# Attention and routed expert layers in one kernel: the attention stage reordered, its evictions widened to two banks, and some transposes moved from TensorE to the DMA queues

## The chip, the cores and the metric

The kernel runs on one core of one Trainium2 chip. The metric is the device time of one execution in microseconds (us). Five runs of the kernel before gave a median of 749.58 us (748.85 to 750.01). The profiled executions that are quoted have a span, first to last instruction, of about 2 us less than the time.

## The reference, cut to what matters

Two parts follow each other. Block attention with a learned mixing of the blocks of keys and values comes first:

```python
B, H, S, D = 4, 8, 768, 64          # 32 heads, handled as 16 pairs; 8 blocks of 96 rows
P = sort_net                         # 8x8 per head
for _ in range(5):                   # five times: max, exp, normalise rows, normalise columns
    P = np.exp(P - P.max(-1, keepdims=True))
    P = P / (P.sum(-1, keepdims=True) + 1e-09)
    P = P / (P.sum(-2, keepdims=True) + 1e-09)
k_sorted = einsum('bhij,bhjcd->bhicd', P, k_blocks)     # and v_sorted likewise
attn = softmax(q_blocks @ k_sorted.T / sqrt(D))
attn_out = attn @ v_sorted
```

Its output, transposed to 3072 rows of 512, feeds eight experts of which every row uses all, weighted by a matrix that is normalised eight times:

```python
P = exp(x @ w_gate - max);  8 x: rows to 1, columns to 1, times N / E
out = sum over e of P[:, e] * (relu(x @ w1[e]) @ w2[e])     # N 3072, D 512, F 1024, E 8
```

The expert layers are 3072 matmuls of 128x128 weights on 512 columns. They dominate.

## The kernel before: the parts that matter

A step `m` of the attention stage works on four pairs at once, each one stage further: it sorts keys and values of pair m and transposes its queries, takes scores of pair m-1, mixes values for pair m-2, and transposes the result of pair m-3. From step 7 on the first batch is complete and expert blocks (`fill`) stand between the stages. Until then a filler matmul (`spin`) stands there.

```python
    def bank(shape, dt=F32):                     # one PSUM bank, eight in rotation
        return ps.tile(shape, dt, name="bank")

    for it in range(5):                          # prologue, 32x64 each, VectorE and ScalarE in turn
        nc.scalar.activation(out=P, in_=P, func=AF.Exp)
        ...
            nc.vector.tensor_tensor(out=Prep, ...)          # last: 32x1024, every entry 16 times
    # [cut: 8 small matmuls, Pbig, R of pair 0 on VectorE]

    def fill(n, both=True):
        for _ in range(n):
            ...
            if last_batch[c] > state["done"]:
                if state["done"] < 0:
                    spin(1)                      # a matmul whose result nobody reads
                return
            h_block(e, c, fb, both)              # 4 matmuls of 512 columns and a relu
            state["h"] += 1

    for m in range(NPAIR + 4):
        if m < NPAIR:
            stage1(m)          # K: 12 matmuls, V: 12, Q: 12 transposes; each bank evicted by itself
        # [cut: loads of pair m+4, expert weights]
        fill(1)
        if 1 <= m <= NPAIR:
            stage2(m - 1)      # scores: 16 matmuls, 4 exponentials of 96x384; V: 8 transposes
        fill(1)
        if 2 <= m <= NPAIR + 1:
            stage3(m - 2)      # mix: 16 matmuls, 4 x (reciprocal, product) on VectorE
        fill(1)
        # [cut: gate]
        if 3 <= m <= NPAIR + 2:
            stage4(m - 3)      # output: 8 transposes, one copy on ScalarE
        fill(1)
        if m >= 6 and m % 4 == 2:
            state["done"] = m // 4 - 1
```

The softmax here doesn't subtract the row's maximum and nothing guards it: scores larger than these inputs give would overflow.

## Time and profile before

| What | us | Where it is read |
|---|---|---|
| span | 747.3 | head of the page |
| TensorE (PE) busy | 736.2 (99%) | page, part 1 |
| first attention matmul | 14.35 | timeline |
| start of step 7, from where expert work fills every gap | 42.42 | timeline |
| first second-layer matmul, after attention and routing | 145.61 | timeline |
| one second-layer tile, 8 matmuls of 512 columns | 1.727 | distance of VectorE's evictions in the timeline |

From the page of the kernel before: the line of busy times of part 1 and the first line of part 4, the chain that ended last.

```profile
PE 736.2 (99%) x4588; PEld 357.4 (48%) x4588; DVE 252.0 (34%) x497; ACT 274.2 (37%) x497; POOL 48.9 (7%) x71
...
PE 98%; DMA 1%; POOL 1%; DVE 0%; issue 0%; POOLq 0%
```

TensorE is the engine that everything waits for, so what counts is the order of time on TensorE. The next fence is from the windows view of the kernel before (columns: stretch in us, its length, busy time and instructions of PE, PE weight loads, VectorE = DVE, ScalarE = ACT, GpSimd = POOL, then the granted clock, the busy share of the DMA engines and GB/s).

```profile
10.00:15.00 5.00, 1.04 (x22) 1.06 (x24) 3.32 (x11) 0.34 (x2) 3.66 (x6) 0.64 1.30 198
15.00:20.00 5.00, 5.00 (x83) 3.12 (x81) 2.31 (x5) 2.40 (x6) 3.75 (x6) 0.68 1.43 199
30.00:40.00 10.00, 9.98 (x219) 7.86 (x215) 9.38 (x29) 8.49 (x20) 6.68 (x10) 1.00 1.31 203
```

Two things stand out. From 10 to 20 us the granted clock is 0.64 and 0.68, so TensorE ran at half speed for part of it (the first K, at 14.35 us, took 0.59 us to the start of V, the next, at 18.23 us, 0.36). And from 30 to 40 us VectorE is busy for 9.38 of 10 us while TensorE is busy for all of it, but partly with fillers. Here is step 5 of the kernel before (steps count from 0), TensorE's rows of the timeline, two fillers left out (start in us, modelled duration, matmuls merged by line; L171 sorts keys and values, L182 transposes queries, L197 are scores, L204 the V transposes, L216 the mix, L227 the output transposes, L266 fillers):

```profile
33.99 0.53 PE L171 MATMUL bank<-R,kb 128*64 128x128 bf16 x12
34.35 0.50 PE L171 MATMUL bank<-R,vb 128*64 128x128 bf16 x12
34.69 0.50 PE L182 MATMUL bank<-ident,qb 128*64 128x128 bf16 x12
35.12 0.39 PE L266 MATMUL bank<-wide 128*128 128x512 bf16 x1
35.44 0.56 PE L197 MATMUL bank<-QT,KT 64*96 64x96 bf16 x16
35.93 0.65 PE L204 MATMUL bank<-ident,VT 128*96 128x128 bf16 x8
...
36.63 0.87 PE L216 MATMUL bank<-vs,at 96*96 96x65 bf16 x16
37.34 0.38 PE L266 MATMUL bank<-wide 128*128 128x512 bf16 x1
37.56 0.50 PE L227 MATMUL bank<-ident,OG 96*128 96x96 bf16 x8
```

The modelled durations overlap; what a group costs TensorE is the distance from its start to the next start. Here that is 0.36 us for K, 0.34 for V, 0.43 for Q, 0.49 for scores and 0.48 for V transposes, 0.71 for the mix, 0.34 for the output: 3.15 us of 4.22. The rest is fillers and gaps.

### The profile page before, as it was taken

What the parts mean: (1) busy time and instruction counts of PE and PEld (TensorE: products, weight loads), DVE (VectorE), ACT (ScalarE), POOL (GpSimd) and SP (SyncE); (2) the same over time, 40 slices, a digit from 0 to 9 for tenths busy, and PEclk for the clock granted to TensorE, in tenths of its full rate; (3) what the DMA queues carried; (4) which work ended last, traced back from release to release, by engine and by line L of the source; (5) the groups of instructions that cost most, each with busy time, mean ns of one, the idle gap of its engine ahead of it and who ended that gap; (6) DMA issues with size and microseconds to landing.
All of it is one profiled execution on the core that took longest, in us unless ns stands there. A gap on an engine that the chain in (4) does not pass through costs nothing.

```text
span 747.3 us, 10663 instructions
## 1 busy us (share of the span) xinstructions
PE 736.2 (99%) x4588; PEld 357.4 (48%) x4588; DVE 252.0 (34%) x497; ACT 274.2 (37%) x497; POOL 48.9 (7%) x71
## 2 busy tenths in 40 slices
PE   6999999999999999999999999999999999999997
PEld 3776665444444444444444444444444444444443
DVE  5887776632122122221221221221221222212443
ACT  2867665513423324324324334234233233243000
POOL 8542000000000000000000000000000000000000
PEclk8999999999999999999999999999999999999999
DMA  9999000011300061200330033000330003000133
GB/s 148 204 205 173 11 2 0 1 29 29 56 1 1 0 104 28 38 1 1 56 57 1 0 57 45 13 0 1 57 56 1 1 0 57 1 0 1 43 154 141
DMA packets 29679, 33.21 MB, mean 44 GB/s; under 512 B 1984, under 2 KB 22464, under 8 KB 29632
## 3 DMA queue, kind: packets, MB, share of 16 engines
q0 software_dynamic: 26128, 26.23, 22.4%
q1 hardware_dynamic: 3504, 6.30, 2.2%
q8 instruction: 36, 0.59, 0.3%
q14 instruction: 11, 0.09, 0.0%
HBM read 52.45 MB, written 6.29 MB: 79 GB/s over the span
## 4 chain that ended last, share of the span: by engine, by line
PE 98%; DMA 1%; POOL 1%; DVE 0%; issue 0%; POOLq 0%
PE bank L249 45%; PE bank L339 44%; PE bank L171 2%; PE bank L216 2%; PE bank L204 1%; PE bank L197 1%; PE bank L266 1%; DMA qb<-in_q_dram 1%; PE bank L182 1%; PE bank L227 1%; PE bank L236 0%; POOL kb L87 0%; POOL vb L87 0%; PE bank L321 0%; POOL qb L87 0%; DVE osbl L345 0%
## 5 line engine op out<-in xcount | busy, mean ns | idle before, releaser
L255 ACT ACTIVATE hTs<-bank 128x512 bf16<-128x512 f32 x358 | 213.7, 597 | 371.2 <-PE bank L249 370.4
L249 PE MATMUL bank<-xtT,w1e 128*128 128x512 bf16 x1536 | 346.1, 379 | 0.0
L339 PE MATMUL bank<-w2e,hTs 128*128 128x512 bf16 x1536 | 338.0, 379 | 0.0
L345 DVE SCALAR_TENSOR_TENSOR osbl<-bank,glog,osbl 128x512 f32<-128x512 f32 x168 | 126.2, 751 | 398.7 <-PE bank L339 398.7
L339 PEld LDWEIGHTS <-hTs 128*128 128x128 bf16 x1536 | 150.2, 98 | 181.1
L249 PEld LDWEIGHTS <-w1e 128*128 128x128 bf16 x1536 | 147.9, 98 | 170.3
L342 DVE TENSOR_SCALAR osbl<-bank,glog 128x512 f32<-128x512 f32 x24 | 18.0, 751 | 54.7 <-PE bank L339 54.7
L200 ACT ACTIVATE at<-bank 96x384 bf16<-96x384 f32 x64 | 26.0, 487 | 7.9 <-PE bank L197 7.6
L220 DVE TENSOR_TENSOR OG<-bank,rc 96x256 bf16<-96x256 f32 x64 | 26.9, 421 | 2.2
L95 POOL DMA_DIRECT2D w1e<-in_moe_w_dram x8 | 6.0, 752 | 312.6 <-PE bank L249 312.3
L99 POOL DMA_DIRECT2D w2e<-in_moe_w_dram x8 | 7.1, 887 | 237.6 <-PE bank L339 237.1
L253 DVE TENSOR_SCALAR hTs<-bank 128x512 bf16<-128x512 f32 x26 | 17.8, 683 | 6.1 <-PE bank L249 6.1
L229 ACT COPY xtT<-bank 128x768 bf16<-128x768 bf16 x16 | 12.8, 798 | 14.1 <-PE bank L227 13.7
L176 ACT CAST KT<-bank 128x384 bf16<-128x384 f32 x32 | 13.8, 486 | 7.9 <-PE bank L171 7.8
L216 PEld LDWEIGHTS <-at 96*96 96x96 bf16 x256 | 14.1, 125 | 2.8
L216 PE MATMUL bank<-vs,at 96*96 96x65 bf16 x256 | 14.0, 209 | 0.0
L87 POOL DMA_DIRECT2D kb<-in_k_dram x16 | 11.6, 724 | 17.4 <-PE bank L171 16.2
L178 DVE CAST VT<-bank 128x384 bf16<-128x384 f32 x16 | 8.9, 553 | 10.6 <-PE bank L171 8.2
L207 DVE COPY vs<-bank 96x1024 bf16<-96x1024 bf16 x16 | 11.0, 690 | 4.0 <-PE bank L204 3.7
L219 DVE RECIPROCAL rc<-bank 96x4 f32<-96x4 f32 x64 | 10.9, 171 | 3.7 <-PE bank L216 3.7
L87 POOL DMA_DIRECT2D vb<-in_v_dram x16 | 11.6, 725 | 6.9 <-PE bank L171 3.4
L87 POOL DMA_DIRECT2D qb<-in_q_dram x16 | 11.6, 724 | 2.7 <-PE bank L216 1.2
(57 smaller groups left out, 184.4 us busy)
## 6 DMA issues: line engine op xcount, KB each, us to landing
w1e<-in_moe_w_dram POOLq DMA_DIRECT2D x8, 1024.0 KB, 8.0
w2e<-in_moe_w_dram POOLq DMA_DIRECT2D x8, 1024.0 KB, 8.8
out_dram<-osbl SPq DMA_DIRECT2D x24, 256.0 KB, 2.0
kb<-in_k_dram POOLq DMA_DIRECT2D x16, 192.0 KB, 7.4
vb<-in_v_dram POOLq DMA_DIRECT2D x16, 192.0 KB, 7.4
qb<-in_q_dram POOLq DMA_DIRECT2D x16, 192.0 KB, 7.4
P<-in_sort_net_dram SPq DMA_DIRECT2D x1, 8.0 KB, 1.6
wg<-in_moe_w_gate_dram POOLq DMA_DIRECT2D x1, 8.0 KB, 6.7
```

Source lines behind the costliest of these rows:

```text
L87: nc.gpsimd.dma_start(out=t, in_=src[2 * m:2 * m + 2].rearrange("h p kk d -> p h kk d"))
L171: nc.tensor.matmul(b_[64 * h2:64 * h2 + 64, k3, :], src[:, h2, 3 * kh2 + k3, :], R[:, h2].rearrange("p i c -> p (i c)"), start=True, stop= ...
L176: nc.scalar.copy(dst, b_)
L200: nc.scalar.activation(out=ATT[m][h2][:, half, :], in_=bb[h2].rearrange("k i q -> k (i q)"), func=AF.Exp, scale=scale)
L216: nc.tensor.matmul(b_[:, i4, :], ATT[m][h2][:, half, 96 * i4:96 * i4 + 96], VS[m][:, i, h2, :], start=True, stop=True)
L220: nc.vector.tensor_tensor(out=OG[m][:, 4 * half:4 * half + 4, h2, :], in0=b_[:, :, 0:64], in1=mkap(rc, [rc.ap[0], [1, 4], [0, 64]]), op=AL ...
L249: nc.tensor.matmul(b_, w1t[e][:, kk, fb * 128:(fb + 1) * 128], xf[:, kk, c * 512:(c + 1) * 512], start=(kk == 0), stop=(kk == 3))
L253: nc.vector.tensor_scalar_max(hT[e, c][:, fb, :], b_, 0.0)
L255: nc.scalar.activation(out=hT[e, c][:, fb, :], in_=b_, func=AF.Relu)
L339: nc.tensor.matmul(b_, hT[e, c][:, fb, tt * 128:(tt + 1) * 128], w2t[e][:, fb, :], start=(fb == 0), stop=(fb == 7))
L342: nc.vector.tensor_scalar(out=osbl[:, t, :], in0=b_, scalar1=glog[:, t, e:e + 1], scalar2=None, op0=ALU.mult)
L345: nc.vector.scalar_tensor_tensor(out=osbl[:, t, :], in0=b_, scalar=glog[:, t, e:e + 1], in1=osbl[:, t, :], op0=ALU.mult, op1=ALU.add)
```

## The change

Its intent is to shorten all that is not expert work: a shorter prologue with the clock kept up, cheaper evictions in steps 0 to 6 and no fillers after step 1, and for the last six pairs fewer transposes on TensorE. The diff, cut to its core:

```diff
+    QA = 2; MB = 10; XB = 10; VA = 3            # [written on lines of their own]
+    SPIN = [(1, 1, 1, 1)] * 2 + [(0, 0, 0, 0)] * 5
+    PROG = ["KF0VFSvF1XQF"] * 7 + ["KVQFSvF01FXF"] * 3 + ["VKQFSvF01FXF"] * 10
-    ps = ... bufs=8 ...                          # one tile per bank
+    PS = ps.tile([128, 8, 512], F32)             # all of PSUM, bank() and bank2() slice it
+    def bank2():                                 # two neighbouring banks
+        turn[0] += turn[0] % 2
+        b_ = PS[:, turn[0] % 8:turn[0] % 8 + 2, :]
...
-    nc.vector.reduce_max(out=rs, in_=P, axis=AX.X)      # and the subtraction
+        if it == 2:
+            q_turn(0, "act")                     # query transposes of pairs 0 and 1 in the prologue
+            spin(12)
+        if it == 4:
+            q_turn(1, "act")
+            spin(8)
-            nc.vector.tensor_tensor(out=Prep, ...)       # 32x1024
+    nc.tensor.matmul(b_, Pb..., ident[0:32, 0:32], ...)  # transpose, then spread by 8 small matmuls
+    build_r(0, pbp..., nc.vector)                        # R of pairs 0 and 1; from pair 2 on: nc.gpsimd
...
+        b2 = bank2().rearrange("d f x -> d (f x)")       # K and V: one eviction of 768 columns
+            nc.scalar.copy(T[:, 0:VA], b2[:, 0:VA])      # V: half each
+            nc.vector.tensor_copy(T[:, VA:6], b2[:, VA:6])
...
+        else:                                            # m >= MB: V sorted by 2 matmuls of 384 columns,
+            vd[m] = drp.tile([6, 128, 128], BF16, ...)   # written to DRAM and read back turned
+            nc.sync.dma_start(out=vd[m]..., in_=VR...)
...
+            nc.scalar.activation(out=ATT[m][h2], in_=bb[h2], func=AF.Exp, scale=scale)   # 96x768
...
+    def x_back(m):                                       # m >= XB: output to DRAM, back transposed
+            nc.sync.dma_start_transpose(out=xr[m], in_=xd[m])
...
+    early = [..., (0, 1, 0, 256), (1, 1, 0, 256), (0, 1, 256, 512), (1, 1, 256, 512), ...]  # half blocks
...
+            y_tile(e, c, tt, 2 if n == len(seq) - 1 and tt == 3 else 1)    # last tile in halves
```

The letters of `PROG` are the order within a step: K, V, Q sort and turn, S scores, v V transposes, 0 and 1 the mixes of the two heads, X output, F an expert block or a filler.

## The prediction

> **What bounds the kernel now.** TensorE, almost everywhere. Page part 1: PE busy 736.2 of 747.3 us; chain of waits: PE 98%. In the last tiles (timeline) VectorE evictions follow every 1.7268 us, eight 512-column matmuls, so 215.9 ns each. The 3072 expert matmuls are then 663 us of pure streaming, which the change does not shorten. All gains lie in the other 84 us:
> - Prologue: the first attention matmul starts at 14.35 us (timeline), after five normalisations of about 1.81 us, a 1.21 us Prep, Pbig and R. The windows view shows a granted clock of 0.64 and 0.68 from 10 to 20 us, costing some 1.5 us more.
> - Pairs 0 to 6, no expert work yet: step 7 starts at 42.42 us, the first expert matmul at 43.55. Steps take 4.2 to 4.4 us, of which matmuls about 3.15 (K .36, V .33, Q .43, scores .49, V transposes .49, mix .71, output transposes .34). The rest is 28 filler matmuls and gaps. VectorE is 94% busy from 30 to 40 us, ScalarE 85%: VectorE sets this pace.
> - From step 7 on PE is 100% busy; a step is 6.80 us: 16 expert matmuls (3.45), attention 3.14, gaps 0.2.
> - Tail after the last matmul: about 4 us.
>
> **What the change does.**
> 1. Prologue: no maximum and subtraction (0.45 us), no 1.21 us Prep; two small matmul steps instead; R of pair 0 straight from PSUM; queries first, two transposed while the chain runs; fillers keep the clock up. The Trainium skill ("TensorE: Matmul & The Clock Gate", section "What's actually happening") says an idle array drops to half clock; the 0.64 agrees. First attention matmul near 13.0 us, at full clock.
> 2. Steps 0 to 6: two-bank evictions halve the fixed costs (the 96x384 exp took 487 ns, the 128x512 relu 597; I estimate 0.75 us per 768 columns), R moves to GpSimd, the fillers of steps 2 to 6 go. Estimated per step: VectorE 4.4 to 3.45 us, ScalarE 3.65 to 3.35, TensorE 3.15 plus 0.3 to 0.5 of gaps. Pace 3.6 to 3.8. The loads land at about 1 us each, 3 per pair, plus about 5 for a first-layer weight load, so pair 6 lands near 31 us: close, just not binding. Step 7 starts near 35.8: 6.6 us gained, including item 1.
> 3. Pairs 10 to 15: V transposes (0.49) and output transposes (0.34) leave TensorE for the DMA: 6 x 0.83 = 5.0 us, all critical because PE is full there. The round trips have 6 us and more of slack.
> 4. Costs: 96 expert matmuls become 192 of half width (estimated +0.7 us), some new bank waits.
> 5. Tail: last tile in halves, -0.5 us.
>
> Sum: -6.6 -5.0 +0.7 -0.5 = -11.4 us.
>
> **Predicted: 738.2 us, range 735 to 743. Faster by over 2%: 0.09; within 2%: 0.89; slower: 0.02.**
>
> **What would show it.** First attention matmul at 13.0 us, clock near 1 from 10 to 20; step 7 near 36 us; steps 7 to 9 still about 6.8 us, steps 10 to 15 about 6.0; expert matmuls at 216 ns; PE idle still small.
>
> **What would make it wrong.** The DMA transpose being slow, or the SyncE queue blocking, so that VectorE's copy of the result waits and holds PE; GpSimd behind on R because its load issues stall; loads binding at step 6; more gaps from changing matmul tile shapes more often; half-width matmuls costing more than half.

## The result

| | median us | range | runs |
|---|---|---|---|
| before | 749.12 | 748.79 to 750.01 | 13 |
| changed | 740.82 | 739.47 to 741.62 | 7 |

The ratio is 0.9884 (95% interval 0.9874 to 0.9894). It is the mean time of one kernel's fast runs over that of the other's of the same rounds, so not quite the ratio of the medians. The record lists an eighth run of the changed kernel, 743.18 us at a mean clock of 0.995, also called fast, which the median of seven leaves out; the median of all eight would be the same, but this run lies just above the forecast range. The gain is 8.3 us of the medians, clear of noise and within 2%. The time lies within the forecast range of 735 to 743; the forecast gain was 11.4 us.

The same two lines of the changed kernel's page:

```profile
PE 730.8 (99%) x4523; PEld 361.8 (49%) x4523; DVE 239.4 (32%) x425; ACT 271.3 (37%) x460; POOL 62.2 (8%) x96
...
PE 97%; DMA 1%; DVE 1%; issue 0%; POOL 0%; ACT 0%; POOLq 0%; DVEq 0%; ACTq 0%
```

The busy share says nothing: it was 99% and is 99%. Two of the three stretches in the changed kernel:

```profile
10.00:15.00 5.00, 4.08 (x55) 2.44 (x55) 2.37 (x9) 1.48 (x2) 2.37 (x5) 1.00 1.30 197
...
30.00:40.00 10.00, 9.74 (x210) 8.04 (x210) 8.84 (x19) 7.93 (x12) 8.39 (x13) 1.00 1.28 204
```

The clock is now 1.00, and VectorE is busy for 8.84 instead of 9.38 us although steps are shorter. This is step 3 of the changed kernel (L222 sorts keys or values, L284 is the mix of one head, L264 scores, L274 V transposes, L317 output, L147 queries), a step that nothing disturbed:

```profile
22.77 0.53 PE L222 MATMUL PS<-R,kb 128*64 128x128 bf16 x12
23.23 0.55 PE L284 MATMUL PS<-vs,at 96*96 96x65 bf16 x8
23.70 0.53 PE L222 MATMUL PS<-R,vb 128*64 128x128 bf16 x12
24.16 0.60 PE L264 MATMUL PS<-QT,KT 64*96 64x96 bf16 x16
24.81 0.61 PE L274 MATMUL PS<-ident,VT 128*96 128x128 bf16 x8
...
26.11 0.53 PE L147 MATMUL PS<-ident,qb 128*64 128x128 bf16 x12
26.46 0.50 PE L222 MATMUL PS<-R,kb 128*64 128x128 bf16 x12
```

The step takes 3.69 us. K and V now cost 0.46 each: about 0.1 us more, since a group of another tile shape follows each of them. (Not every change of shape costs this: the mix of the second head takes 0.34 us before the output, less than the first takes before V.) Scores cost 0.65 instead of 0.49, though the V transposes follow them in both kernels. That is at least partly a wait: the V transposes start at 24.81 us, just after VectorE's product of the first mix (24.07 to 24.76 us in VectorE's timeline), whose bank they are next to use. But step 4 took 4.35 us, and step 7 started later than expected. Part of the reason is in these rows of the same view, from steps 4 and 6:

```profile
27.83 0.60 PE L264 MATMUL PS<-QT,KT 64*96 64x96 bf16 x15
29.01 0.24 PE L264 MATMUL PS<-QT,KT 64*96 64x96 bf16 x1 [0.59 <-issue]
...
34.47 0.34 PE L222 MATMUL PS<-R,kb 128*64 128x128 bf16 x6
35.02 0.36 PE L222 MATMUL PS<-R,kb 128*64 128x128 bf16 x6 [0.20 <-issue]
```

The sixteenth score matmul and the second half of K came late, and the profile names no engine that they waited for ("issue").

Two points on TensorE, the start of step 7 and the first second-layer matmul (141.29 us in the changed kernel), divide the two traces into three stretches, which account for the whole difference of the spans, 747.3 and 739.0 us. The changed kernel runs one expert block (0.96 us) at the end of step 6; its first stretch is counted to the start of that block. With it, it runs four expert blocks more (16 matmuls at 215.9 ns, 3.45 us) before the second layer; they are taken from the second stretch and added to the third.

| Stretch | before | changed | gain | forecast |
|---|---|---|---|---|
| start to step 7 | 42.42 | 39.60 - 0.96 = 38.64 | 3.8 | 6.6 |
| step 7 to the first second-layer matmul | 103.19 | 102.65 - 3.45 = 99.20 | 4.0 | 5.0 - 0.7 = 4.3 |
| the second layer to the end | 601.7 | 597.7 + 3.45 = 601.2 | 0.5 | 0.5 |

So the forecast missed by 2.8 us in the first stretch, and nearly nowhere else. That the second stretch fits is partly luck: there the DMA route gave about 0.7 us less than forecast and the half-width blocks cost about 0.4 us less (experiment 1), and these two misses nearly cancel.

### The profile page after: what moved, and what is told of

It reads as the page before. It is cut to its first block, busy times and chain, and to the rows that moved or that the text cites. A ratio compares the mean times of both kernels' runs of the same rounds, so it can differ in the third digit from the quotient of the medians.

```text
span 739.0 us, 10546 instructions
## 1 busy us (share of the span) xinstructions
PE 730.8 (99%) x4523; PEld 361.8 (49%) x4523; DVE 239.4 (32%) x425; ACT 271.3 (37%) x460; POOL 62.2 (8%) x96
## 4 chain that ended last, share of the span: by engine, by line
PE 97%; DMA 1%; DVE 1%; issue 0%; POOL 0%; ACT 0%; POOLq 0%; DVEq 0%; ACTq 0%
PE PS L339 45%; PE PS L454 45%; PE PS L284 2%; PE PS L222 1%; PE PS L264 1%; DMA qb<-in_q_dram 1%; PE PS L274 1%; PE PS L147 1%; PE PS L138 0%; PE PS L317 0%; PE PS L326 0%; PE PS L244 0%; DVE OG L288 0%; PE PS L432 0%; DVE VT L230 0%
## 5 line engine op out<-in xcount | busy, mean ns | idle before, releaser
L345 ACT ACTIVATE hTs<-PS 128x512 bf16<-128x512 f32 (+1 forms) x372 | 215.1, 579 | 390.8 <-PE PS L339 389.9
L339 PE MATMUL PS<-xtT,w1e 128*128 128x512 bf16 (+1 forms) x1632 | 345.6, 366 | 0.0
L454 PE MATMUL PS<-w2e,hTs 128*128 128x512 bf16 x1544 | 337.9, 378 | 0.0
L460 DVE SCALAR_TENSOR_TENSOR osbl<-PS,glog,osbl 128x512 f32<-128x512 f32 (+1 forms) x169 | 126.4, 748 | 398.3 <-PE PS L454 398.2
L457 DVE TENSOR_SCALAR osbl<-PS,glog 128x512 f32<-128x512 f32 x24 | 18.0, 751 | 51.2 <-PE PS L454 51.2
L343 DVE TENSOR_SCALAR hTs<-PS 128x512 bf16<-128x512 f32 (+1 forms) x36 | 20.4, 570 | 15.7 <-PE PS L339 15.6
L268 ACT ACTIVATE at<-PS 96x768 bf16<-96x768 f32 x32 | 24.2, 802 | 1.6 <-PE PS L264 0.9
L288 DVE TENSOR_TENSOR OG<-PS,rc 96x512 bf16<-96x512 f32 x32 | 22.0, 686 | 1.1
L227 ACT CAST KT<-PS 128x768 bf16<-128x768 f32 x16 | 12.8, 798 | 8.1 <-PE PS L222 7.1
L284 PEld LDWEIGHTS <-at 96*96 96x96 bf16 x256 | 14.2, 125 | 2.1
L284 PE MATMUL PS<-vs,at 96*96 96x65 bf16 x256 | 14.9, 210 | 0.0
L264 PE MATMUL PS<-QT,KT 64*96 64x96 bf16 x256 | 9.3, 209 | 0.6 <-issue 0.6
L264 PEld LDWEIGHTS <-KT 64*96 64x96 bf16 x256 | 7.2, 121 | 4.8 <-issue 4.3
```

The lines of the kernel that those rows point to most:

```text
L227: nc.scalar.copy(T, b2)
L264: nc.tensor.matmul(bb[h2][:, i // 4, 96 * (i % 4):96 * (i % 4) + 96], KT[m][hs, i].rearrange("d kk c -> d (kk c)"), QT[m][hs, :, 16 * i:16 ...
L268: nc.scalar.activation(out=ATT[m][h2], in_=bb[h2], func=AF.Exp, scale=scale)
L284: nc.tensor.matmul(b_[:, i // 4, i % 4, :], ATT[m][h2][:, i // 4, 96 * (i % 4):96 * (i % 4) + 96], VS[m][:, i, 65 * h2:65 * h2 + 65], star ...
L288: nc.vector.tensor_tensor(out=OG[m][:, :, h2, :].rearrange("q (f i) d -> q f i d", f=2), in0=b_[:, :, :, 1 - h2:65 - h2], in1=mkap(rc, [rc ...
L339: nc.tensor.matmul(b_, w1t[e][:, kk, fb * 128:(fb + 1) * 128], xf[:, kk, c * 512 + lo:c * 512 + hi], start=(kk == 0), stop=(kk == 3))
```

## The experiments

The expectations below call the step that starts at 26.46 us step 5; counted from 0, as everywhere else here, it is step 4. Each kernel was timed in five rounds against the kernel before, which gave medians of 749.27 to 749.55 us, so the changed kernel's 740.82 us can stand beside them. Starts of steps are from the one profiled execution of each.

### 1. All transposes back on TensorE

```diff
-    MB = 10
-    XB = 10
+    MB = 16
+    XB = 16
```

> The changed kernel with all sixteen pairs turned on TensorE (nothing through the DMA). Theory: on a full TensorE the moved transposes are worth what the steps show, 0.33 us per V and 0.36 us per output, 6 of each: about +4.1 us, so 744.9 us. Rival 1, the prediction's own figure of 0.83 us per pair: +5.0, 745.8. Rival 2, the round trips cost what they save: 740.8, no change.

Measured: 745.26 us (744.47 to 746.25), 4.4 us slower than the changed kernel, about half of the whole gain. The stretch from step 7 to the second layer, counted from the expert block of step 6 (38.64 us in the changed kernel, 39.87 here), is 4.26 us longer in its trace. The rows of its end, first from the changed kernel's timeline, then from this one's:

```profile
141.29 9.01 PE L454 MATMUL PS<-w2e,hTs 128*128 128x512 bf16 x41
...
146.79 3.40 PE L454 MATMUL PS<-w2e,hTs 128*128 128x512 bf16 x14
```

So the DMA route does give about what the steps show. Steps 11, 13 and 14 of the changed kernel take 6.47, 6.13 and 6.12 us; here they take 6.84, 6.84 and 6.83. Without the DMA route this stretch is 0.3 us longer than in the kernel before (106.91 against 103.19 + 3.45 = 106.64), so the half-width blocks and all else that is new there cost about 0.3, not the 0.7 us forecast for the blocks alone. In the routing stretch of the changed kernel 24 half-width matmuls took 2.62 us, where 12 full ones took 2.59.

A V turn is worth 0.33 us (step 11 against step 10, 6.80 us, in the changed kernel) to 0.37 us (step 11 of the two kernels), and not 0.49, because two groups got longer. In the changed kernel the two wide V matmuls take 0.42 us where twelve narrow ones took 0.34, and the mix takes 0.82 instead of 0.71. The second of these is a bank wait. These rows are of step 11 of the changed kernel, all engines:

```profile
70.26 1.50 ACT L268 ACTIVATE at<-PS 96x768 bf16<-96x768 f32 x2 [0.15 <-PE PS L264]
...
70.99 0.87 PE L284 MATMUL PS<-vs,at 96*96 96x65 bf16 x16
...
71.81 1.03 PE L339 MATMUL PS<-xtT,w1e 128*128 128x256 bf16 x8
```

ScalarE's two exponentials read the scores' banks until 71.76 us; the expert block after the mix (71.81) starts as they end and would be the next user of one of them. The V transposes used to stand between, and their 0.49 us hid that wait.

### 2. The kernel before without its later fillers, and the changed kernel with them

```diff
 # kernel before
-                if state["done"] < 0:
+                if state["done"] < 0 and state["m"] < 2:
                     spin(1)
 # changed kernel
-    SPIN = [(1, 1, 1, 1)] * 2 + [(0, 0, 0, 0)] * 5
+    SPIN = [(1, 1, 1, 1)] * 7
```

> The kernel before, without fillers after step 1 (21 fewer filler matmuls, 4.5 us of TensorE). Theory, as the prediction had it: VectorE sets the pace of steps 3 to 6, they stay at 4.1 to 4.4 us, and the time falls by less than 1.5 us from 749.1. Rival, from TensorE's ledger: the fillers themselves were the cost, steps fall to about 3.5 us and the time falls by 4 to 5 us.

> The changed kernel with the fillers of steps 2 to 6 put back: 20 filler matmuls, 4.3 us of TensorE. Theory: in the changed kernel TensorE's own work and its gaps set these steps (3.67 us), not VectorE or ScalarE, so the fillers come on top; they also slow the rate of instructions, so the stalls of steps 5 and 6 (1.2 us in all, no other engine waited for) go: net about +3.1 us, 743.9. Rival 1: the stalls do not depend on the rate of instructions: +4.3 us, 745.1. Rival 2: another engine still sets the pace: the fillers hide, within 1 us of 740.8.

Measured: the kernel before without these fillers took 748.82 us (748.28 to 749.25; ratio 0.9992, 0.9978 to 1.0006): no difference. The changed kernel with them took 744.7 us (744.18 to 746.8), 3.9 us slower. (The program takes away 20 fillers and puts back 19, 4.3 and 4.1 us, not 21 and 20 as the expectations have it.) So the fillers were free before and would not be free now. A ledger of TensorE alone would have said that removing fillers won the time: it shows 52 of them before and 38 after. That reading falls. The next fence has the windows view of the kernel before without fillers, for three of its steps (columns as above).

```profile
28.70:41.85 13.15, 11.16 (x255) 10.08 (x254) 12.41 (x39) 10.71 (x24) 9.31 (x13) 1.00 1.28 204
```

Two rows of TensorE's timeline from these steps of the same kernel:

```profile
34.02 0.53 PE L171 MATMUL bank<-R,vb 128*64 128x128 bf16 x12 [0.43 <-ACT xtT L229]
...
35.87 0.61 PE L204 MATMUL bank<-ident,VT 128*96 128x128 bf16 x8 [0.32 <-ACT at L200]
```

VectorE is busy for 12.41 of 13.15 us (94%), TensorE for 11.16, and the steps still take 4.37 to 4.39 us. V (34.02) and the V transposes (35.87) now stand idle for banks that others have yet to empty. So TensorE was not the limit of these steps. VectorE's own work is 12.41 / 3 = 4.14 us a step, so without cheaper work on VectorE no order of the other engines could have brought them below that. But the two waits shown name ScalarE, whose copy (L229) waits for TensorE in turn (0.6 us in the waits view), so a chain of ScalarE and TensorE may hold the last 0.25 us of a step; no run separates the two. What made steps of 3.67 us possible is the cheaper eviction: 96x512 products at 686 ns replaced twice as many of 96x256 at 421 ns, and R (about 0.42 us) left VectorE. No run undid these evictions alone, so this is read from the two traces.

In the changed kernel the fillers come on top, because TensorE with its gaps is now the limit. They cost more per step than their 0.86 us (4.93 to 4.98 us against 3.67), for two reasons that the trace shows: a filler adds changes of tile shape (queries take 0.46 us before a filler and 0.35 before K, and a filler 0.31 before K or scores and 0.22 before the mix), and from scores to V transposes it takes 0.86 us instead of 0.65. The sum of 3.9 us lies between the two figures expected. Its profiled run shows no issue stall in steps 2 to 6, as the theory had it, but the same run had a cold array in the prologue (clock 0.66 from 10 to 15 us), so the sum can't be divided closely.

### 3. The last eight fillers of the prologue

```diff
             q_turn(1, "act")
-            spin(8)
```

> The changed kernel without the last eight fillers of the prologue. Theory: these fillers hold TensorE until 12.3 us while the normalised matrix was ready at 11.14 us, so the first attention matmul moves from 13.75 to about 12.6 us and the whole kernel gains 1.1 us. Rival: the arrival of the loads sets steps 5 and 6, step 7 still starts at 39.6 us, gain under 0.4 us. Second rival: the clock falls to half and it gets slower.

Measured: 740.07 us (739.82 to 741.16), 0.75 us below the changed kernel, which is within the scatter of both. The trace shows both halves of the expectation. The first attention matmul came at 12.50 us, 1.25 us earlier. But the clock fell. These are rows of TensorE's timeline in the changed kernel:

```profile
10.13 0.53 PE L147 MATMUL PS<-ident,qb 128*64 128x128 bf16 x12 [1.14 <-DMA qb<-in_q_dram]
10.59 1.90 PE L138 MATMUL PS<-wide 128*128 128x512 bf16 x8
12.41 0.20 PE L184 MATMUL PS<-ident,Pb 32*64 32x32 bf16 x1
...
13.75 0.53 PE L222 MATMUL PS<-R,kb 128*64 128x128 bf16 x12 [0.52 <-DVE R L196]
```

The same view of the kernel without the eight fillers:

```profile
11.16 0.20 PE L183 MATMUL PS<-ident,Pb 32*64 32x32 bf16 x1 [0.51 <-DVE Pb L178]
...
12.50 0.62 PE L221 MATMUL PS<-R,kb 128*64 128x128 bf16 x12 [0.52 <-DVE R L195]
...
14.37 1.46 PE L138 MATMUL PS<-wide 128*128 128x512 bf16 x3
```

In the changed kernel the normalised matrix was ready at 11.14 us, and the matmul that needs it (12.41) stood behind the fillers in TensorE's order, which themselves stood behind the arrival of the second pair's queries (10.13). Without the fillers three later fillers take 1.46 us for what took 0.82, and the windows view gives a clock of 0.78 and 0.88 from 10 to 20 us. All of the gain was lost to that by step 1, which starts at 15.76 us here and at 15.74 in the changed kernel. Step 7 starts 0.8 us earlier all the same, since this run lacks the stall of step 4 (3.67 instead of 4.35 us).

The traces of five kernels whose prologue is that of the changed kernel (the changed kernel itself, a_no_dma, a_va4, a_no_loads and a_early_kvq) have the first attention matmul 3.62 us (once 3.63) after the start of the query transposes of pair 1, which wait for a load in four of them (a_va4, the earliest, shows no wait). That start was at 9.20, 9.50, 9.57, 10.13 and 10.88 us. A sixth, a_fill, had 5.16 us since its array was cold; the expectation of experiment 7 says six traces, and should have said five. So the end of the prologue follows these transposes, and mostly the landing of a load. This is likely why the changed kernel's times scatter over 2.2 us (3.7 with the eighth run), more than those of the kernel before (1.2 us over 13 runs); experiment 7 takes this wait away.

### 4. V's eviction split on the bank border

```diff
-    VA = 3
+    VA = 4
```

> The changed kernel with V's eviction split at 4 of 6 blocks, so that each engine reads a PSUM bank of its own. Theory: VectorE's half waits for ScalarE's half now (6.4 us of waits in total) because both read one bank; with the split on the bank border the two run side by side and that wait goes. Steps 3 to 6 (3.66 us) are set by TensorE's own work and gaps, so the time stays within 0.5 us of 740.8. Rival: this serial eviction is on the critical path of each step, then steps shrink by 0.2 to 0.4 us and the time falls by 1.5 to 2.5 us.

Measured: 741.15 us (740.18 to 742.35): no difference. The wait did go. With three blocks each, both engines read the first bank, and VectorE waited for ScalarE's half. From the waits view of the changed kernel (us in total, times, longest):

```profile
DVE VT L230 <- ACT VT L229: 6.4, 5, 1.6
```

In this run the same instructions overlap, as the timeline has it (the second row starts before the first ends, and what VectorE waits for before it is TensorE):

```profile
16.07 0.59 ACT L229 CAST VT<-PS 128x512 bf16<-128x512 f32 x1
16.16 0.42 DVE L230 CAST VT<-PS 128x256 bf16<-128x256 f32 x1 [1.56 <-PE PS L222]
```

The Trainium skill ("PSUM — Partial Sum Buffer", section "PSUM bank collisions raise a hardware error") says that two engines may not use one bank on the same partitions at once, reads included, and that software has to order them. The order that appears here agrees with it: one shared bank, and the second reader waits until the first is done. Its going changed the time by no more than the scatter: the five waits stand in steps 0, 1 and 7 to 9, and not in steps 2 to 6. In steps 7 to 9 expert work fills TensorE; step 1 took 3.10 instead of 3.36 us.

### 5. Fewer loads (wrong on purpose)

```diff
     def load(src, m):
+        if m >= 6:
+            qkv[id(src), m] = qkv[id(src), m - 5]      # reuse, so the result is wrong
+            return
```

> Wrong on purpose: the changed kernel whose pairs 6 to 15 reuse the buffers of earlier pairs, so 30 of the 48 loads of queries, keys and values are not made and the DMA queues are quiet sooner. Theory: the stalls of steps 5 and 6 end about 1.45 us after TensorE's fetch of instructions, which stands behind these loads; with fewer loads steps 5 and 6 take 3.67 us, step 7 starts 1.2 to 1.8 us earlier and the time falls as much, to about 739.4. Rival 1: the stalls come from the number of instructions per us and not from the loads: no change. Rival 2: loads or GpSimd set the pace of all steps: steps 2 to 4 also fall under 3.5 us.

Measured: 740.09 us (739.49 to 740.76; result wrong, as meant). Step 4 took 4.69 us and K of step 6 was slow again (0.68 instead of 0.43 us). Step 7 started 0.43 us earlier than in the changed kernel, which is less than the 0.63 us by which its prologue happened to be earlier. The theory falls: the stalls do not come from the loads. What they come from is narrowed by four things that the traces show.

- They stand at fixed instructions. In the changed kernel and in a_no_dma and a_va4, K of step 6 breaks after its 6th matmul; in the two kernels of experiment 6, whose prologue has three fillers fewer, it breaks after the 9th; in c3_q1_later (experiment 7), which has five matmuls more before this point, after the 1st. The rows of c1_fillers_order's timeline:

```profile
33.83 0.44 PE L224 MATMUL PS<-R,kb 128*64 128x128 bf16 x9
34.65 0.30 PE L224 MATMUL PS<-R,kb 128*64 128x128 bf16 x3 [0.37 <-issue]
```

- Each of nine such stalls, in six kernels, ends 1.3 to 1.6 us after a packet of 16,384 bytes on an instruction queue (q8) has landed (DMA records of the trace; in the changed kernel 27.62 and 33.70 us, with the stalls ending at 29.01 and 35.02). These packets are about 6 us apart in steps 4 to 7.
- In the changed kernel 127 matmuls, each with its weight load, lie between the two stalls: 254 instructions. The Trainium skill ("Runtime: NRT & Kernel Launch", section "Instruction fetch mechanics") says that an engine's instructions come in blocks of 16 KiB, 256 instructions each, over a DMA queue of its own. Packet size and distance agree with it, and so does the count: the profile has 35 packets on that queue, and 4523 matmuls with their weight loads are 35.3 times 256 instructions. It also says that crossing into a new block is mostly hidden; here it was not.
- The stalls are absent in the kernel before, whose steps took 4.2 to 4.4 us for about the same instructions, and in steps 2 to 6 of a_fill. They are nearly absent in steps 2 to 6 of a_no_spin8 too, whose undisturbed pace is that of the changed kernel (3.67 to 3.69 us a step). There the border would stand eight matmuls later, and the packets landed at 27.40 and 33.38 us, a little earlier. So the pace alone does not make a stall; how far ahead the packets are counts too.

An undisturbed step of the changed kernel has 84 matmuls in 3.67 us, so 127 of them would take 5.5 us, less than the 6 us from packet to packet. That fits steps which ask for TensorE's instructions a little faster than they arrive. But 6 us need not be the shortest distance: in a_no_loads two packets landed 3.7 us apart (33.14 and 36.85 us), and what sets the distance was not tested. All of this points to the fetch, but no run changed the fetch alone, so it is argued and not shown; and why a stall ends 1.3 to 1.6 us after a packet stays open. In the changed kernel the stalls are 4.35 - 3.67 = 0.7 us in step 4 and 0.4 us in step 6, where K took 0.83 instead of 0.43 us.

### 6. Two mendings, and turning from pair 8

The first kernel has all of these edits but the last, the second all of them:

```diff
-            spin(8)
+            spin(2)
     ...                                       # matmul of the normalised matrix
+    spin(1)
     ...                                       # the 8 small matmuls
+    spin(2)
-    ... ["VKQFSvF01FXF"] * 10
+    ... ["VKQFSvFF01XF"] * 10                 # two expert blocks between scores and mix
-    MB = 10; XB = 10                          # second kernel only, and the new order from step 8
+    MB = 8; XB = 8
```

> The changed kernel with two mendings: the eight fillers before the normalised matrix become two before it, one and two around the small matmuls after it, and from step 10 on two expert blocks instead of one stand between scores and mix. Theory: first attention matmul at 12.5 us with the clock kept at full speed (1.25 us earlier), and the mix of steps 11 to 16 at 0.71 instead of 0.82 us since its bank is then free: together -1.9 us, of which a longer instruction stall may take up to 1 us: 739 to 740. Rival: mix is longer for another reason and stays at 0.82.

> The kernel of c1 with the turns through the DMA from pair 8 on instead of 10. Theory: two more V turns at 0.33 us and two more output turns at 0.36: 1.4 us below c1, about 738. Rival: the DMA queues are still full until 65 us, so the round trips come late and VectorE or the mixes wait: no gain or slower than c1.

Measured: 739.56 us (738.97 to 741.93; ratio 0.9876, 0.9862 to 0.9891) for the first, so not separable from the changed kernel. The mix is back at 0.70 us, so it was the bank wait. But the steps hardly shrank (10 to 14 together 32.41 instead of 32.59 us): V and Q next to the moved blocks got longer. And the array was still cold for part of the prologue (clock 0.66 from 10 to 15 us), for the second pair's queries were waited for before the fillers.

The second kernel took 741.5 us (741.22 to 742.32; ratio 0.9898, 0.9884 to 0.9911). Its median is 1.9 us above that of the first, though the two intervals overlap a little. The rival was right that round trips come late and VectorE waits, and the trace shows it; that the queues full until 65 us are the reason is not shown, for the wait ends at 80.14 us. From the waits view of this kernel, 44 to 125 us:

```profile
DVE xtT L314 <- DMA xr<-xd: 2.2, 1, 2.2
PE PS L147 <- DVE hTs L345: 2.1, 1, 2.1
```

From TensorE's timeline of the same kernel:

```profile
78.21 0.53 PE L224 MATMUL PS<-R,kb 128*64 128x128 bf16 x12
80.88 0.53 PE L147 MATMUL PS<-ident,qb 128*64 128x128 bf16 x12 [2.15 <-DVE hTs L345]
81.34 1.79 PE L341 MATMUL PS<-xtT,w1e 128*128 128x256 bf16 x8
```

VectorE's copy of a transposed pair waited 2.2 us for its DMA transpose; the relu behind it on VectorE came late, its bank was not free, and TensorE stood for 2.15 us and then ran at half speed for a while (8 half-width matmuls took 1.72 instead of 0.98 us). An off-TensorE route is free only as long as its result is there when the in-order engine reaches it.

### 7. The second pair's queries out of the prologue; the early order

The last three kernels try the order of later steps in steps 0 to 6; a prologue that waits for no second load, together with the order of experiment 6 and V turned through the DMA from pair 8 on; and both.

```diff
 # a_early_kvq
-    PROG = ["KF0VFSvF1XQF"] * 7 + ...
+    PROG = ["KVQFSvF01FXF"] * 7 + ...
 # c3_q1_later (against the first kernel of experiment 6)
-    QA = 2; MB = 10
+    QA = 1; MB = 8                            # outputs stay at XB = 10; order of c2
-            q_turn(1, "act")
-            spin(2)
+            spin(10)
 # c4_both: c3 with "KVQFSvF01FXF" in steps 2 to 6
```

> The changed kernel with the order of steps 0 to 6 as in later steps: K, V, Q together, then scores, V transposes, both mixes, output transposes. Theory: K took 0.36 and V 0.34 us when matmuls of one tile shape stand together and 0.46 each when mixes stand between; fewer changes of shape make a step 3.4 to 3.5 instead of 3.67 us, five steps give 1.0 us, so 739.8, unless the instruction stalls (which stand at fixed instructions of TensorE) grow by as much. Rival: in this order the mixes wait for the banks that ScalarE's exponentials still read, as in the kernel before without fillers (4.39 us a step): slower than 740.8.

> c1 with the second pair's query transposes moved from the prologue to step 1, ten fillers in their place, and V turned through the DMA from pair 8 on, outputs from pair 10 on. Theory: in six traces of the changed prologue the first attention matmul comes 3.62 us after the second pair's queries arrive, which varies from 9.5 to 11.7 us; without that wait it comes at 12.5 us at full clock in every run, spread of the times under 1 us; two more V turns give 0.66 us; 738.3 us. Rival: VectorE waits for late round trips as in c2, 740 or more.

> c3 with steps 2 to 6 in the order of a_early_kvq. Theory: whatever that order gives or costs adds to c3: 737.3 if it is worth 1 us, 738.3 if the instruction stalls take it back, more if the bank waits bite.

Measured: the early order alone took 742.34 us (741.8 to 744.69), slower than the changed kernel, and with the new prologue 740.58 us (740.5 to 740.88). The rival was right that it is slower, but not in its reason: the longest waits are of the queries and the V transposes for VectorE, and not of the mixes for ScalarE. Groups of one shape stand together, but TensorE waits. Two rows of step 5 in the first of them:

```profile
32.38 0.53 PE L147 MATMUL PS<-ident,qb 128*64 128x128 bf16 x12 [0.26 <-DVE OG L288]
...
33.90 0.61 PE L274 MATMUL PS<-ident,VT 128*96 128x128 bf16 x8 [0.46 <-DVE VT L230]
```

The order of the changed kernel, with its mixes pulled apart and its 0.1 us gaps, is worth more than it costs: steps 3 and 5 take 3.69 and 3.66 us, and not 4.42 and 4.26.

The kernel with the new prologue and the old early order (c3_q1_later) took 738.61 us (738.38 to 739.03; ratio 0.9858, 0.9844 to 0.9871). This interval does not meet that of the changed kernel (0.9874 to 0.9894), and its four timed runs lie within 0.65 us. In its trace TensorE is busy from 10 to 15 us without a gap at full clock (windows view):

```profile
10.00:15.00 5.00, 5.00 (x59) 2.44 (x57) 3.00 (x11) 1.18 (x2) 3.45 (x8) 1.00 1.29 196
```

Its first attention matmul comes at 12.66 us (TensorE's timeline):

```profile
6.40 5.00 PE L138 MATMUL PS<-wide 128*128 128x512 bf16 x22
11.33 0.20 PE L183 MATMUL PS<-ident,Pb 32*64 32x32 bf16 x1
...
12.66 0.53 PE L223 MATMUL PS<-R,kb 128*64 128x128 bf16 x12
```

It beats both kernels: 10.9 us below the kernel before of its own rounds, where the changed kernel gains 8.3. The new prologue is only part of it. Of the 2.2 us between the two traces (spans 739.0 and 736.8), 1.0 lie before the expert block of step 6 (37.60 instead of 38.64 us) and 1.0 between it and the second layer (101.68 instead of 102.65), where V now leaves TensorE from pair 8 on and the blocks are moved.

## Why the prediction was right, and where its sum was off

- **TensorE bounds the kernel; 216 ns per expert matmul is fixed.** Right. Tiles of the second layer follow at 1.727 us before and after, and the last stretch differs only by its tail. The Trainium skill ("TensorE: Matmul & The Clock Gate", section "Wait — 56ns, not 53.3ns?") gives 215.7 ns for 512 columns at full clock; the traces agree with 215.9.
- **VectorE sets the pace of steps 3 to 6 before.** Right that TensorE does not: without fillers the time is the same (experiment 2). VectorE's own 4.14 us a step is a floor under those steps; whether it or a chain with ScalarE holds the last 0.25 us is not shown.
- **Prologue, "First attention matmul near 13.0 us, at full clock".** The clock was right: 1.00. The time was 13.75 us in the profiled run and varies. The term missed that fillers stand in TensorE's order behind a load and in front of the chain (experiments 3 and 7). Off by about 0.75 us.
- **"Pace 3.6 to 3.8".** Right for undisturbed steps: 3.66 to 3.69, with TensorE and its gaps, some of them short waits for VectorE, as the limit.
- **"Step 7 starts near 35.8: 6.6 us gained, including item 1."** This is the term that failed: 38.64 us and 3.8 us gained. Of the 2.8 us, 0.75 are the prologue and about 1.1 the stalls in steps 4 and 6, which the prediction did not have. The rest, about 1.0 us, is a remainder and is not shown by a run. Most of it lies in steps 0 to 2, which have fewer stages but took 1.99, 3.36 and 3.67 us; the trace has fillers in the first two, and V transposes that wait 0.28 us for VectorE in step 1. The warning that loads would bind at step 6 did not come true (experiment 5).
- **"6 x 0.83 = 5.0 us" for the DMA route.** The mechanism was right and the critical path too. The size was 4.3 to 4.4 us (experiment 1), since a V turn was worth 0.33 to 0.37 and not 0.49: wide V matmuls took 0.08 us more and the mix waited 0.11 us for a bank.
- **"estimated +0.7 us" for half-width matmuls.** About 0.3 us.
- **"The round trips have 6 us and more of slack".** Right for pairs 10 to 15. The margin is not large: with outputs turned from pair 8 on VectorE waited (experiment 6). The Trainium skill ("DMA: Bandwidth & Descriptors", section "DMA Transpose (X-bar)") has the plain DMA transpose issued by Sync or Scalar only; here SyncE issues all six, and the profile's table of issues gives a median of 3.7 us from issue to landing.
- **Tail, -0.5 us.** Right: 0.5.

The range held because two misses, in the first stretch, were of the kind it allowed for. The middle was 2.6 us too low.

## What to carry to other kernels

Before pricing the removal of filler work on the busy engine, ask whether another engine sets the pace there: 4.3 us of fillers were free before, and 4.1 us of them cost 3.9 us after the evictions had become cheaper. A filler that keeps the clock up belongs where the engine waits anyway and never behind a load and in front of the critical chain; moved so, it gave about 1.0 us of c3_q1_later's gain as its trace has it, and the four times of that kernel lie within 0.65 us. When a transpose leaves the full engine, count what its time was hiding (here a bank still being read), and check that the copy of its result stands late enough in the order of the engine that makes it.

## What the Trainium skill lacked or had wrong

- "TensorE: Matmul & The Clock Gate" puts the fall to half clock at an idle window of about 3.4 us. Shorter gaps came before it here: one of 2.01 us in the prologue of a_fill (clock 0.66 from 10 to 15 us) and one of 2.15 us in the second kernel of experiment 6, while one of 1.51 us in a_no_dma left the clock at 1.00. Without the eight fillers the array idled for 1.14 us and then for pieces of 0.51, 0.27 and 0.52 us around short matmuls, and the clock was 0.78 from 10 to 15 us. The page does say, of another kernel, that frequent short idles between groups make the clock swing; it names no lengths for them.
- "TensorEngine Tiling (Array Packing)" says that a change of tiling mode drains TensorE, and gives no time for it. Groups that took 0.36 and 0.34 us when one of their own tile shape followed took 0.46 when another followed; whether these shapes are modes in the page's sense no run shows.
- "Runtime: NRT & Kernel Launch" calls the crossing of a 16 KiB block of instructions mostly hidden. In steps of 84 matmuls in 3.67 us, TensorE stood for 0.2 to 0.9 us at fixed instructions 127 matmuls apart, without a releaser, and went on 1.3 to 1.6 us after a 16,384-byte packet on the instruction queue. That the fetch is the cause is likely and not shown.
